# Two attention layers on one core: part of the second layer laid out by another planner's clock, its values joined to the next head's scores, V's weights asked earlier

## The chip, the cores and the metric

One NeuronCore of a Trainium2 chip. The time is device microseconds of one execution of the program. Each kernel is run several times and its median is compared; a profiled execution gives the spans of every instruction.

## The reference

Two independent attention layers on 2048 rows of 1024 numbers, float32, 32 heads of 32. Both project `x` to Q, K and V and the result by `wo`; the two outputs are put side by side.

```python
def _A_ref(x, wqkv, wo):            # W, dil = 8, 2: each row sees itself and 7 rows at steps of two before it
    ...
    idx = pos[:, None] - off[None, :]
    mask = idx >= 0
    ...
    logits = jnp.einsum("bhsd,bhswd->bhsw", q, kg) * scale
    logits = jnp.where(mask[None, None, :, :], logits, -1e9)
    attn = _softmax(logits, axis=-1)
    o = jnp.einsum("bhsw,bhswd->bhsd", attn, vg)
    return (lambda x, *d: x.transpose(*d))(o, 0, 2, 1, 3).reshape(B, S, D) @ wo

def _B_ref(x, wqkv, wo):            # W = 256: each row sees itself and the 255 rows before it
    ...
    scores = jnp.einsum("bhqd,bhkd->bhqk", q, k) * (Dh ** -0.5)
    mask = (idx[:, None] - idx[None, :] >= 0) & (idx[:, None] - idx[None, :] < W)
    scores = jnp.where(mask[None, None], scores, -1e9)
    o = jnp.einsum("bhqk,bhkd->bhqd", _softmax(scores, axis=-1), v)
    ...
```

## The kernel before

The rows come in eight units of 512: units 0 to 3 are layer B ("dense"), units 4 to 7 layer A ("window"; its even and odd rows are separate sequences, so that the dilation becomes a plain window of eight). `DU` is 4, the first unit of layer A. A unit has eight groups of four heads; `hg = 8 * u + s` numbers them through, so layer A has groups 32 to 63. In this text a "head" of layer A is such a group.

**Large matmuls.** Every float32 operand of a projection is split in two fp32r parts (`parts`, L247: a cast on ScalarE or VectorE, L249 or L252, and a subtraction on VectorE, L255), and three products of parts are added, so that one block of contraction is three matmuls of 128x128 by 128x512. A Q/K block `("qk", u, s)` is 2 halves of 8 such steps k, 48 matmuls. V comes in parts: `("v", u, 0)` covers four groups, in two rounds of four weight blocks, 12 matmuls a block. In units 6 and 7 V, and after all units layer A's output, are formed from seven products of sums (`("vp", ...)`, `("p", ...)`), in place of eight. Layer A's sums are made in the background: loads, additions on VectorE (L1073), stores. The items of these products that are sums of inputs are of kind "xw".

**Weights.** The class `Stream` holds all weights and inputs in one list in the order of use. `load_to` fetches the next 512 KB into a raw buffer, by GpSimd's DMA queue (L194), when a split has freed one; `split_to(n)` queues the splits up to item n. Who calls `split_to` and when is set by hand in the blocks: in a Q/K block at certain steps k (L660 to L677), in a V block through `ahead` (L745). Three split weights and three raw buffers are held.

**Small matmuls.** In layer A a head's scores are 64 matmuls of 32x32 by 32x40 in plain float32, each two passes, so 128 matmuls and 128 weight loads. VectorE and ScalarE make the softmax (`mask`, `top`, `total`, L1178 to L1216), transpose it and spread it into `wide` (`spread`, L1218); then the values are 16 or 20 matmuls, 32 or 40 passes. Before, a head's Q and K rows go from TensorE through a buffer (`nat`, three of them) by SyncE's queue into one of two seats (`evac_window`, L555). In the trace the seats bear the name of the buffer that they lie in, `pbuf`.

**The order.** Nothing is decided at run time: a planner in the program text lays out the instructions of every engine. `Clock` (L63) keeps a time for each engine with durations written into it. The loop from L1576 on has four lists: `a` (small helpers), `2` (second passes and values), `1` (scores) and `g` (large matmuls), and takes the item that can start first by the clock. An item's `ready` gives the time from which it can start, or None. Work of the other engines is emitted when the clock reaches it (`defer`).

TensorE's instructions are counted as they are laid out (`issued`; four for a float32 matmul, two for a split one), and `asked` notes when the clock thinks that the next 256 were requested. `short(n)` (L299) says that a burst of n instructions would outrun those that are there; the dispatcher then takes a large matmul instead, if one can start. `Clock.move` (L126) places DMA transfers one after the other on one server.

Of the kernel before, what the change touches and what calls it, by code (L numbers as in the profile page):

```python
# [29 lines left out]
CHUNK, ASKED, LEFT, FETCHED = 256, 150, 290, 7.0  # L30
EXTRA, EACH = 246, 5.2
P_LATE = 1.5
VPARTS = ((0,4),(4,2),(6,2))
V_SLOTS = {0:0,5:1,7:2}
O_SLOTS = {2: (0, 1), 3: (2, 3), 4: (4, 5), 5: (6, 7)}
# [17 lines left out]
CW = 1.36  # L53
# [9 lines left out]
class Clock:  # L63
# [10 lines left out]

    def __init__(self):
        self.free = dict(pe=0.0, act=0.0, dve=0.0, pool=0.0, sp=0.0)
        self.port = dict(dve=0.0, pool=0.0)
        self.later, self.lands, self.busy = [], [], []
        self.n = 0

    @property
# [3 lines left out]
    def start(self, eng, port, *ready):  # L85

        t = max((self.free[eng],) + ready)
        if eng == "pool":
            t = max(t + 0.06, self.port["dve"])
        elif port:  # L90
            t = max(t, self.port["pool"])
        return t
# [4 lines left out]
    def use(self, eng, dur, *ready, port=False):  # L97
        end = self.free[eng] = self.ends(eng, dur, *ready, port=port)
        if eng == "pool" or port:
            self.port[eng] = end  # L100
        return end + self.SEEN[eng]

    def issue(self, eng, kind, *ready):
        start = max((self.free[eng],) + ready) + (0.28 if eng == "pool" else 0.0)
        self.free[eng] = start + self.HOLD[eng]
        return self.move(start + self.LEAD[eng], *self.MOVE[kind])

    def copy(self, kind, *ready):

# [16 lines left out]
    def move(self, t, dur, tail):  # L126

        busy = self.busy = [x for x in self.busy if x[1] > self.now - 20.0]
        i = 0
        while i < len(busy):  # L130
            if busy[i][1] <= t or busy[i][0] < t:
                t = max(t, busy[i][1])
            elif busy[i][0] - t >= dur:
                break
            else:
                t = busy[i][1]
            i += 1
        busy.insert(i, (t, t + dur))
        return t + dur + tail

    def defer(self, t, f):
# [123 lines left out]
def kernel(ctx, tc, xs, wqk, wv, wo, outs, units):  # L265
# [31 lines left out]
        nc.tensor.matmul(out, left, right, **k)  # L297

    def short(n):  # L299
        return ck.now < asked[1] + FETCHED and issued[0] + EXTRA + n > asked[0] * CHUNK + ASKED + LEFT  # L300


    plan = []
# [21 lines left out]
    sx = dram.tile([P, 4, 4, S], F32, name="sx")  # L325
    vd = dram.tile([P, 4, S], F32, name="vd")
    done = {}
    for k in ("stack", "v", "o", "ot", "out", "nat", "second", "clear", "scores", "s", "t", "vs", "vw", "vd"):
        done[k] = {}
    gates = {}  # L330

# [208 lines left out]
    def qk_items(u, s):  # L540
# [14 lines left out]
        def evac_window(t, ps, bank):  # L555
            if t == 0:
                h2["qk"] = natp.tile([P, 2 * S + 16], F32R, tag="nat", name="nat").bitcast(F32)[:, :2 * S + 8]
                nc.scalar.activation(h2["qk"][:, :S], ps, AF.Copy, scale=SCALE)
                e = ck.use("act", 0.485, ck.now + ck.SEM)
                by_head(0, S, e)  # L560
            else:
                qk = h2["qk"]
                nc.scalar.copy(qk[:, S + 8:], ps)
                e = ck.use("act", 0.485, ck.now + ck.SEM)
                nc.scalar.copy(qk[:, S:S + 8], tails[:, s, :])
                e = ck.use("act", 0.2, e)
                if u + 1 < U and not units[u + 1][3]:
                    ck.defer(e + 1.0, lambda: (nc.vector.memset(tails[:, s, :], 0.0), ck.use("dve", 0.08, ck.now)))
                if u + 1 < U and units[u + 1][3]:
                    nc.scalar.copy(tails[:, s, :], ps[:, S - 8:])  # L570
                    e = ck.use("act", 0.2, e)
                by_head(S, 2 * S + 8, e)
            rg.give(bank, e)
# [65 lines left out]
        for t in range(2):  # L639
            h = {}  # L640

            def ready(k, t=t, h=h):
                if k == 0:
                    st.split_to(where["qk", u, s, t] + 1)
                    w = st.ready[where["qk", u, s, t]]
                    h["r"] = w if isinstance(w, list) else [w, w]
                    return latest(rg.when(), h["r"][0], xready[u][0])
                if k >= len(xready[u]):
                    return None
                if k == NK - 1 and nat + t >= NN and (dense or t == 0):  # L650
                    n = done["nat"].get(nat + t - NN)
                    return n and max(xready[u][k], n - 0.6)
                return max(xready[u][k], h["r"][k // 4])

            def run(k, t=t, h=h):
                if k == 0:
                    h["ps"], h["b"] = rg.take()
                    h["w"], _ = st.get(where["qk", u, s, t])
                for i, (a, b) in enumerate(TERMS):
                    mm(h["ps"], h["w"][:, a, k * P:(k + 1) * P], xt[u][k][:, b, :],  # L660
                                     start=(k == 0 and i == 0), stop=(k == NK - 1 and i == 2))
                then = where["qk", u, s, t] + 1
                if t == 1 and s == 0 and u:
                    then = max(then, st.split)
                kinds = [kind for kind, _ in st.items[then:then + 2]]
                if k == ASK and kinds and kinds[0] not in ("x", "xw"):
                    st.split_to(then + 1)
                if k == ASK and t == 0 and u > DU and kinds[:1] == ["x"] and st.split >= where["qk", u, s, 1]:
                    st.split_to(where["qk", u, s, 1] + 1)
                if kinds[:1] == ["xw"] and k in (0, 2, 4, 6):  # L670
                    st.split_to(then + 1 + k // 2)
                if kinds == ["w", "w"] and k == 5 and (then in firsts or then + 1 in firsts):
                    st.split_to(then + 2)
                if kinds == ["w", "xw"] and k == 6:
                    st.split_to(then + 2)
                if k in (4, 6) and kinds[:1] == ["xt"]:
                    st.split_to(then + k // 2)  # L677
                if k == 6 and t == 1 and not hg:
                    st.split_to(7)

            def after(k, t=t, h=h):
                if k == NK - 1:
                    evac(t, h["ps"], h["b"])

            for k in range(NK):
                out.append((lambda k=k, ready=ready: ready(k), lambda k=k, run=run: run(k), 3 * CG,
                            lambda k=k, after=after: after(k)))
# [12 lines left out]
    def v_items(u, part):  # L700
# [11 lines left out]
        def item_of(i):  # L712
            return where["v", u, part, i]
# [12 lines left out]
        def run(r, n, k, b):  # L726
# [15 lines left out]
            done_block = k == kw - 1 and b == 1  # L742
            if wide and r == 0:
                if k == 0 and b == 1 and n < 3:
                    ahead(item_of(n + 1))  # L745
            elif wide:
                if done_block and n == 0:
                    ahead(item_of(4))
                if k == 0 and b == 1 and n == 3:
                    ahead(item_of(4) + 1)  # L750
            elif k == 1 and b == 0:
                ahead(item_of(n) + 1)

        def ahead(i):
            if st.items[min(i, len(st.items) - 1)][0] != "x":
                st.split_to(i + 1)
# [388 lines left out]
    def window(u, s):  # L1145
# [16 lines left out]
        h = {}  # L1162

        def scores_ready():
            return latest(rs.empty(), done["stack"].get((u, s)),
                          done["clear"].get(buf) if hg - 2 <= last_dense else done["o"].get(hg - 2))

        def scores():
# [49 lines left out]
        def spread(e):  # L1218
            turned = band[buf][:, 1024:].rearrange("p (j b t c) -> p j b t c", j=4, b=4, t=2)
            diag = wide[buf].rearrange("p j (b c) -> p j b c", b=4)  # L1220
            for i in range(4):
                r, c = 32 * i, 32 * i + 8
                nc.scalar.copy(diag[r:r + 32, :, :, c:c + 32], turned[r:r + 32, :, :, 1, :])  # L1223
                ck.use("act", 0.632, e)
                n, c = ((i - 1) * 32, c) if i else (96, 0)
                nc.scalar.copy(diag[n:n + 32, :, :, c:c + 8], turned[r:r + 32, :, :, 0, :8])
                h["p"] = ck.use("act", 0.31, e)

        def values_ready():
            return latest(done["v"].get((u, vp)), h.get("p") and h["p"] + P_LATE, ro.when())  # L1230

        def values():
# [10 lines left out]

            return after

        return [Item(scores_ready, scores, CW, 256)], [Item(values_ready, values, C3 + 0.9, 16 * len(kbs))]

    def free_keys(hg):

# [274 lines left out]
            twos += b  # L1524
    xt[0], xready[0] = [], []
    x1 = None
    for p in plan:
        if p[0] == "qk":
            new = qk_items(p[1], p[2])
            if p == ("qk", 0, 0):  # L1530
# [45 lines left out]
    while True:  # L1576
# [16 lines left out]
        if ck.later and (best is None or ck.later[0][0] < best[0]):  # L1593
# [2 lines left out]
            ck.flush(t)  # L1596
            continue
        t, name = best
        it = seqs[name][pos[name]]
        pos[name] += 1  # L1600
        ck.free["pe"] = t
# [49 lines left out]
```

## Time and profile before

| what | value |
|---|---|
| runs | 1799.02, 1805.24, 1803.62 us; median 1803.62 us |
| profiled execution | 1800.08 us, span 1798.4 us |
| TensorE matmul busy | 1775.5 us (99%) |
| VectorE, ScalarE, GpSimd busy | 1298.0, 940.8, 410.6 us |
| layer A's bursts of scores | from 1046 to 1648 us |
| output products | from about 1637 us to the end |

PE is TensorE's matmuls, PEld its weight loads, DVE VectorE, ACT ScalarE, POOL GpSimd, SP SyncE. In the names, `g` is the bank of a large matmul, `s` that of scores and `o` that of values; `x`, `w` and `r` are split inputs, weights and sums (the buffers of the latter have the name `r`). Matmuls overlap in the array, and their ends are modelled by the profiler, so the length of one record is not the time that it costs; the chain of waits and the distance of starts tell that.

### The profile page before, as it was taken

Reading aid. Unit: us, or ns where it says so; the run is one execution under the profiler, and the core shown is the slowest. Engines: PE = TensorE matmul, PEld = TensorE weight load, DVE = VectorE, ACT = ScalarE, POOL = GpSimd, SP = SyncE. Lnnn points to the kernel's source line nnn. Section 1 sums busy time; section 2 is a strip of 40 time slices with the busy share of each in tenths; the row PEclk is TensorE's granted clock in tenths of the full one; section 3 lists DMA queues with packets and bytes.
Section 4 is the critical chain, followed back from the end, with each engine's and each line's share of the span. In section 5 each row is a group of like instructions: output and inputs, shape, how many; then the busy total and the mean of one; then the engine's idle time right before and its main releaser. Section 6 shows DMA issues by size and latency. Waiting matters only on the chain.

```text
span 1798.4 us, 38453 instructions
## 1 busy us (share of the span) xinstructions
PE 1775.5 (99%) x14496; PEld 1440.0 (80%) x14496; DVE 1298.0 (72%) x2887; ACT 940.8 (52%) x2336; POOL 410.6 (23%) x952
## 2 busy tenths in 40 slices
PE   9999999999999999999999999999999999999999
PEld 7787777888777888778788778877887787777887
DVE  6777876768867769867678476756666768689866
ACT  5565566555656565655655444534544435355442
POOL 3322323222342223332223400100010101001120
PEclk9999999999999999999999999999999999999999
DMA  8354664645646556555546265766566568868984
GB/s 257 105 148 136 185 167 135 170 136 141 185 141 166 153 132 170 146 152 149 144 128 173 83 194 180 213 211 186 160 219 203 185 183 280 265 182 270 356 286 144
DMA packets 154794, 324.58 MB, mean 180 GB/s; under 512 B 18032, under 2 KB 58992, under 8 KB 154608
## 3 DMA queue, kind: packets, MB, share of 16 engines
q0 software_dynamic: 45792, 166.74, 30.4%
q1 hardware_dynamic: 98736, 137.02, 26.8%
q10 hardware_dynamic: 10080, 18.35, 2.7%
q8 instruction: 115, 1.88, 0.4%
q14 instruction: 71, 0.58, 0.1%
HBM read 201.33 MB, written 53.48 MB: 142 GB/s over the span
## 4 chain that ended last, share of the span: by engine, by line
PE 89%; DVE 3%; issue 3%; DMA 3%; ACT 2%; POOL 0%; SPq 0%; DVEq 0%; ACTq 0%; POOLq 0%
PE g L297 70%; PE s L297 13%; PE o L297 6%; DMA raw<-xs 1%; DVE w L255 1%; DVE x L255 0%; ACT s L1361 0%; DMA pbuf<-nat 0%; ACT w L249 0%; DVE band L1212 0%; DMA raw<-wqk 0%; DVE sm L1208 0%; DMA qst<-nat 0%; DMA raw<-wv 0%; DVE r L979 0%
## 5 line engine op out<-in xcount | busy, mean ns | idle before, releaser
L297 PE MATMUL g<-x,w 128*128 128x512 f32 x3552 | 879.9, 394 | 4.9 <-DVE x L255 3.1
L297 PEld LDWEIGHTS g<-x,w 128*128 128x128 f32 x3552 | 655.6, 188 | 135.1 <-issue 7.9
L255 DVE TENSOR_TENSOR w<-raw,w 128x512 fp32r<-128x512 f32 x510 | 334.4, 697 | 45.1 <-ACT w L249 39.0
L1361 ACT ACTIVATE s<-s,nm 128x384 f32<-128x384 f32 (+2 forms) x512 | 274.4, 537 | 106.7 <-DVE nm L1356 100.2
L1356 DVE CUSTOM_DVE_ANT_0 s<-s,mask_d 128x384 f32<-128x384 f32 (+2 forms) x512 | 262.0, 554 | 93.1 <-PE s L297 92.8
L297 PE MATMUL g<-w,x 128*128 128x256 f32 (+1 forms) x1728 | 307.7, 327 | 1.3 <-DVE w L255 0.9
L1420 POOL TENSOR_SCALAR_AFFINE_SELECT pbuf<-pbuf 128x128 f32<-128x128 f32 (+1 forms) x603 | 218.8, 391 | 318.9 <-ACT pbuf L1441 317.2
L297 PEld LDWEIGHTS g<-w,x 128*128 128x128 f32 x1728 | 255.3, 190 | 26.4 <-DVE w L255 2.1
L297 PE MATMUL g<-r,w 128*128 128x512 f32 x960 | 239.0, 393 | 1.1 <-issue 0.6
L1441 ACT ACTIVATE pbuf<-s 128x384 f32<-128x384 f32 (+2 forms) x480 | 203.3, 505 | 65.8 <-PE s L297 64.1
L297 PEld LDWEIGHTS g<-r,w 128*128 128x128 f32 x960 | 177.2, 188 | 36.6 <-issue 1.4
L194 POOL DMA_DIRECT2D raw<-wqk x126 | 68.6, 544 | 395.7 <-DVE w L255 256.4
L297 PEld LDWEIGHTS s<-qst,kst 128*128 128x128 f32 x704 | 113.9, 189 | 42.6 <-ACT s L1361 16.8
L297 PE MATMUL s<-kst,qst 96*128 96x384 f32 (+2 forms) x512 | 143.0, 343 | 0.9 <-ACT s L1361 0.7
L297 PE MATMUL s<-qst,kst 128*128 128x256 f32 (+2 forms) x704 | 137.4, 302 | 4.0 <-ACT s L1361 3.2
L252 DVE CAST w<-raw 128x1024 fp32r<-128x1024 f32 x173 | 119.7, 692 | 12.3 <-PE g L297 9.0
L249 ACT CAST w<-raw 128x1024 fp32r<-128x1024 f32 (+1 forms) x83 | 85.8, 1038 | 69.8 <-PE g L297 28.0
L297 PEld LDWEIGHTS s<-kst,qst 96*128 96x128 f32 x512 | 93.7, 189 | 26.6 <-issue 4.4
L1361 ACT ACTIVATION_READ_ACCUMULATOR s<-s,nm 128x1 f32 x512 | 105.3, 206 | 0.0
L1223 ACT COPY wide<-band 32x512 f32<-32x512 f32 x128 | 79.0, 617 | 32.0 <-DVE band L1214 30.4
L297 PE MATMUL o<-pbuf,vbuf 128*32 128x384 f32 (+2 forms) x1408 | 91.1, 388 | 0.0
L255 DVE TENSOR_TENSOR x<-raw,x 128x512 fp32r<-128x512 f32 x116 | 75.4, 689 | 19.8 <-ACT x L249 18.5
(90 smaller groups left out, 1390.8 us busy)
## 6 DMA issues: line engine op xcount, KB each, us to landing
raw<-wqk POOLq DMA_DIRECT2D x126, 512.0 KB, 4.6
raw<-wv POOLq DMA_DIRECT2D x60, 512.0 KB, 4.8
qst<-nat SPq DMA_DIRECT2D x96, 256.0 KB, 6.0
kst<-nat SPq DMA_DIRECT2D x96, 256.0 KB, 5.5
raw<-wo POOLq DMA_DIRECT2D x44, 512.0 KB, 4.3
raw<-xs POOLq DMA_DIRECT2D x28, 512.0 KB, 4.7
outs<-ost ACTq DMA_DIRECT2D x38, 256.0 KB, 3.2
kst<-halo SPq DMA_DIRECT2D x72, 128.0 KB, 4.7
```

Source lines behind the costliest of these rows:

```text
L194: (self.nc.scalar if early else self.nc.gpsimd).dma_start(raw if len(ap.shape) == 2 else raw.rearrange("p (a b) -> p a b", a=2), ap)
L249: nc.scalar.copy(t[:, 0, :], raw)
L252: nc.vector.tensor_copy(t[:, 0, :], raw)
L255: nc.vector.tensor_tensor(t[:, 1, c:c + 512], raw[:, c:c + 512], t[:, 0, c:c + 512].bitcast(F32), op=ALU.subtract)
L297: nc.tensor.matmul(out, left, right, **k)
L1223: nc.scalar.copy(diag[r:r + 32, :, :, c:c + 32], turned[r:r + 32, :, :, 1, :])
L1356: nc.vector.tensor_tensor_reduce(ps[:, :n], ps[:, :n], mask[:, cut:full], scale=-1.0, scalar=BIG, op0=ALU.add, op1=ALU.min, accum_out=nm)
L1361: nc.scalar.activation(ps[:, :n], ps[:, :n], AF.Exp, bias=nm, scale=-1.0, accum_out=sm)
L1420: nc.gpsimd.affine_select(w, w, pattern=[[0, m], [step, n]], compare_op=ALU.is_ge, fill=0.0, base=base, channel_multiplier=chan)
L1441: nc.scalar.activation(w, ps[:, :pack * n].rearrange("p (j n) -> p j n", j=pack), AF.Exp)
```

## The change

It alters the order in which instructions are laid out, and which engine clears a small tile; the arithmetic is the same.

- **Clock.** While the large matmuls from `("qk", 4, 2)` to the first output product are laid out, `ck.traced` is on. GpSimd's own instructions are then placed around the intervals in which VectorE holds the shared port. A transfer goes through `share`: two queues (GpSimd's, and the others), each first in first out; where both have one under way, each moves at half speed. A 512 KB load has a duration of 1.5 us and a tail of 0.76, before 2.12 and 0.14.
- **Joined values.** For heads below `PAIRED` = 50: the scores of a head wait until the probabilities of the head before are spread, and the values of a head wait until the scores of the next are laid out. The scores' instruction count takes in the 64 or 80 of the values.
- **`short`.** More than 7 us after a request it no longer returns "not short" but counts one more packet of 256 as there.
- **V.** In round 0 of `("v", u, 0)`, for units 4 and 5, the split of block n + 2 is asked at block n, before of block n + 1.
- **"xw" items.** Asked at earlier steps of the Q/K block ahead of them.
- **Tails.** In unit 5 the eight clearings of a group's tail columns go from VectorE to GpSimd.

```diff
@@ class Clock
         t = max((self.free[eng],) + ready)
-        if eng == "pool":
+        if eng == "pool" and self.traced:
+            t = next((e for s, e in self.held if s <= t + 0.06 < e), t + 0.06)
+        elif eng == "pool":
             t = max(t + 0.06, self.port["dve"])
...
-        return self.move(start + self.LEAD[eng], *self.MOVE[kind])
+        dur, tail = self.MOVE[kind]
+        if self.traced:
+            return self.share(eng, start + self.LEAD[eng], *((1.5, 0.76) if kind == "load" else (dur, tail)))
+        return self.move(start + self.LEAD[eng], dur, tail)
...
+    def share(self, eng, t, dur, tail):
+
+        mine, other = self.moves[eng == "pool"], self.moves[eng != "pool"]
+        t = begin = max(t, mine[-1][1] if mine else 0.0)
+        for s, e in other:
+            if e <= t:
+                continue
+            n = max(s - t, 0.0)
+            if n >= dur:
+                break
+            t, dur = t + n, dur - n
+            n = min((e - t) / 2, dur)
+            t, dur = t + 2 * n, dur - n
+            if not dur:
+                break
+        mine.append((begin, t + dur))
+        del mine[:-60], other[:-60]
+        return t + dur + tail
...
     def short(n):
-        return ck.now < asked[1] + FETCHED and issued[0] + EXTRA + n > asked[0] * CHUNK + ASKED + LEFT
+        there = asked[0] * CHUNK + ASKED + LEFT + (0 if ck.now < asked[1] + FETCHED else CHUNK)
+        return issued[0] + EXTRA + n > there
...
@@ evac_window
-                    ck.defer(e + 1.0, lambda: (nc.vector.memset(tails[:, s, :], 0.0), ck.use("dve", 0.08, ck.now)))
+                    ck.defer(e + 1.0, lambda: (nc.gpsimd.memset(tails[:, s, :], 0.0), ck.use("pool", 0.08, ck.now)))
...
@@ qk_items, run
-                if kinds[:1] == ["xw"] and k in (0, 2, 4, 6):
-                    st.split_to(then + 1 + k // 2)
+                if kinds[:1] == ["xw"] and k in (0, 2, 4):
+                    st.split_to(then + 2 + k // 2)
...
-                if kinds == ["w", "xw"] and k == 6:
+                if kinds == ["w", "xw"] and k == 3:
                     st.split_to(then + 2)
...
@@ v_items, run
                 if k == 0 and b == 1 and n < 3:
-                    ahead(item_of(n + 1))
+                    ahead(item_of(min(n + 2, 3) if u >= DU else n + 1))
...
@@ window
         def scores_ready():
-            return latest(rs.empty(), done["stack"].get((u, s)),
+            if last_dense + 1 < hg < PAIRED and hg - 1 not in done["p"]:
+                return None
+            return latest(rs.empty(), done["stack"].get((u, s)), done["p"][hg - 1] + P_LATE if last_dense + 1 < hg < PAIRED else 0.0,
                           done["clear"].get(buf) if hg - 2 <= last_dense else done["o"].get(hg - 2))
...
         def values_ready():
+            if hg + 1 < PAIRED and hg + 1 not in done["scores"]:
+                return None
             return latest(done["v"].get((u, vp)), h.get("p") and h["p"] + P_LATE, ro.when())
...
-        return [Item(scores_ready, scores, CW, 256)], [Item(values_ready, values, C3 + 0.9, 16 * len(kbs))]
+        return [Item(scores_ready, scores, CW, 256 + (16 * len(kbs) if hg < PAIRED else 0))], [Item(values_ready, values, C3 + 0.9, 16 * len(kbs))]
...
+        if name == "g":
+            ck.traced = marks[0] <= pos["g"] < marks[1]
```

More of the change, by code (lines that the diff above doesn't have):

```diff
@@ L32 @@
 P_LATE = 1.5
+PAIRED = 50
 VPARTS = ((0,4),(4,2),(6,2))
@@ L76, in __init__ @@
         self.free = dict(pe=0.0, act=0.0, dve=0.0, pool=0.0, sp=0.0)
-        self.port = dict(dve=0.0, pool=0.0)
-        self.later, self.lands, self.busy = [], [], []
+        self.port, self.held, self.traced = dict(dve=0.0, pool=0.0), [], False
+        self.later, self.lands, self.busy, self.moves = [], [], [], [[], []]
         self.n = 0
@@ L100, in use @@
             self.port[eng] = end
+        if port:
+            self.held = [x for x in self.held if x[1] > self.now - 5.0] + [(end - dur, end)]
         return end + self.SEEN[eng]
@@ L327 @@
     done = {}
-    for k in ("stack", "v", "o", "ot", "out", "nat", "second", "clear", "scores", "s", "t", "vs", "vw", "vd"):
+    for k in ("stack", "v", "o", "ot", "out", "nat", "second", "clear", "scores", "s", "t", "vs", "vw", "vd", "p"):
         done[k] = {}
@@ L1226, in spread @@
                 nc.scalar.copy(diag[n:n + 32, :, :, c:c + 8], turned[r:r + 32, :, :, 0, :8])
-                h["p"] = ck.use("act", 0.31, e)
+                done["p"][hg] = h["p"] = ck.use("act", 0.31, e)
         def values_ready():
+            if hg + 1 < PAIRED and hg + 1 not in done["scores"]:
+                return None
             return latest(done["v"].get((u, vp)), h.get("p") and h["p"] + P_LATE, ro.when())
@@ L1526 @@
     x1 = None
+    marks = []
     for p in plan:
+        if not marks and p[1:] == (DU, 2) and p[0] == "qk":
+            marks.append(len(gemm))
+        if len(marks) == 1 and p[0] == "p":
+            marks.append(len(gemm))
         if p[0] == "qk":
```

## The prediction

> **What bounds the kernel now.** I read the page first, then the busy time by stretch, then the waits of TensorE in layer A's attention, then the chain of waits and the timeline around each.
>
> ```profile
> span 1798.4 us, 38453 instructions
> PE 1775.5 (99%) x14496; PEld 1440.0 (80%) x14496; DVE 1298.0 (72%) x2887; ACT 940.8 (52%) x2336; POOL 410.6 (23%) x952
> q8 instruction: 115, 1.88, 0.4%
> PE 89%; DVE 3%; issue 3%; DMA 3%; ACT 2%; POOL 0%; SPq 0%; DVEq 0%; ACTq 0%; POOLq 0%
> 1046.00:1393.00 347.00, 343.66 (x4297) 285.56 (x4300) 226.99 (x409) 157.82 (x295) 36.54 (x65) 1.00 0.63 196
> 1393.00:1541.00 148.00, 141.33 (x1648) 112.25 (x1644) 110.90 (x196) 71.04 (x134) 17.32 (x32) 1.00 0.71 226
> 1541.00:1637.00 96.00, 96.00 (x1478) 76.94 (x1477) 69.43 (x119) 43.18 (x85) 9.92 (x19) 1.00 0.65 200
> ```
>
> The first numbers of a stretch are its length and TensorE's busy time. TensorE (PE) is busy 99% of the span and holds 89% of the chain, so no other engine's busy time is for sale: a change can only remove TensorE's own work or its idle time. The diff removes no matmul. Up to the third Q/K block of unit 4 it changes one thing, how early V's weights are asked in unit 4; the clock is back to the old one where the output products begin, near 1637 us. The stretches between hold 347.00 - 343.66 = 3.3, 148.00 - 141.33 = 6.7 and 0.0 us of idle time: 10.0 us in all. That is the ceiling for every wait that the change could take away; only joined bursts can add to it.
>
> Who ended those waits (1046 to 1669 us; total, times, longest):
>
> ```profile
> PE g L297 <- DVE x L255: 2.9, 2, 2.3
> PE g L297 <- DVE w L255: 2.6, 6, 0.8
> PE g L297 <- issue: 1.6, 2, 1.0
> PE g L297 <- DVE w L252: 1.0, 1, 1.0
> PE o L297 <- issue: 0.9, 1, 0.9
> PE s L297 <- issue: 0.5, 1, 0.5
> PE g L297 <- ACT w L249: 0.4, 1, 0.4
> ```
>
> Two kinds: 2.9 + 2.6 + 1.0 + 0.4 = 6.9 us for a split weight (w) or input (x), and 1.6 + 0.9 + 0.5 = 3.0 us for "issue", which means that nothing in the profile releases TensorE.
>
> **Part 1: values joined to the next scores (heads 32 to 48, 17 joins).** Each burst of small matmuls interrupts the large ones. From the chain of waits (start, length):
>
> ```profile
> 1047.79 6.34 PE g L297 x27
> 1054.14 1.16 PE s L297 x101
> 1055.30 0.52 issue
> 1063.80 1.05 PE o L297 x32
> 1064.85 1.25 PE s L297 x109
> 1079.16 1.25 PE s L297 x109
> 1083.36 1.05 PE o L297 x32
> 1175.25 1.26 PE s L297 x104
> 1176.51 1.10 PE o L297 x32
> 1669.55 124.72 PE g L297 x549
> ```
>
> Undisturbed, one large matmul takes 124.72 / 549 = 0.227 us. The 27 between two bursts took 6.34 rather than 27 x 0.227 = 6.13: 0.21 us goes to leaving and entering. Apart, scores and values cost 1.25 + 1.05 + 2 x 0.21 = 2.72 us; joined, 1.26 + 1.10 + 0.21 = 2.57. A join saves 0.15 us. In the chain four pairs of such bursts already lie against each other (the first at 1063.80, the last at 1356), so 13 joins are new: 13 x 0.15 = **2.0 us**; bounds 0 (the admission rule lets large matmuls in between) and 2.6 (all 17).
>
> The join adds waits: scores of head n+1 wait for the probabilities of head n, and values of n wait for those scores.
>
> ```profile
> 1236.51 1.25 PE s L297 x104
> 1254.45 1.11 PE o L297 x40
> ```
>
> Scores to values of one head took 17.9 us here, and 17 heads in the 347 us stretch make one per 20.4 us, so the chain of one head fits before the next is due. While bursts wait, nothing stands idle: the dispatcher takes large matmuls instead. What is held longer is the seat of a head's Q and K rows and the three buffers before it by at most one head's time. I price that at nothing, since three buffers cover more than one head; if a Q/K block had to wait for its buffer, TensorE would pay directly.
>
> **Part 2: instruction supply.** Three of the "issue" waits lie in heads below 50, one behind it:
>
> ```profile
> 1240.22 1.32 PE L297 MATMUL g<-r,w 128*128 128x512 f32 x5 [0.65 <-issue]
> 1355.66 1.32 PE L297 MATMUL s<-pbuf 32*32 32x40 f32 x128
> 1356.91 0.72 PE L297 MATMUL o<-wide,vbuf 128*32 128x8 f32 x20
> 1358.58 0.88 PE L297 MATMUL o<-wide,vbuf 128*32 128x136 f32 x20 [0.94 <-issue]
> 1483.99 2.88 PE L297 MATMUL g<-x,w 128*128 128x512 f32 x12 [0.97 <-issue]
> ```
>
> All four follow within 3 us of a scores burst: 128 matmuls and 128 weight loads in 1.25 us, where the large ones take 29 us for as many. The instruction queue moved 1.88 MB in 115 packets, and 2 x 14496 instructions over 115 is 252, so a packet is about 256 of TensorE's instructions, one burst. I read these waits as TensorE outrunning that queue. That at 1055.30 is in a second burst 6.34 us behind the first; joined, bursts lie a softmax apart, and it goes (0.5). Those of 0.65 and 0.94 depend on where the burst falls between two packets: the new rule counts values too, and goes on counting after the wait for a packet is over. A pair is 256 + 64 or 80 instructions, though, longer than a packet. Sum 2.1; I take **1.5**, bounds 2.1 and, if pairs starve more than single bursts, well below nothing (the slower rival). The 0.97 lies where heads are no longer joined but the order is new: half, **0.5**.
>
> The Trainium skill (Runtime: NRT & Kernel Launch, Instruction fetch mechanics) also has blocks of 16 KiB, 256 instructions, but says that fetching is mostly hidden because dispatch is slower than the fill. The 0.94 us in the middle of a run that waits for no engine speak against the second half; by that rule this part would be worth nothing, and I take the row.
>
> **Part 3: V asked a block ahead.**
>
> ```profile
> 1172.44 2.81 PE L297 MATMUL g<-w,x 128*128 128x512 f32 x11 [0.66 <-DVE w L255]
> ```
>
> This is unit 5's V, waiting for a split that VectorE put behind a softmax. Asked one block (12 matmuls, 12 x 0.227 = 2.7 us) earlier, it is there: **0.7**, bounds 0 and 0.7. The price: the split can be queued on VectorE or ScalarE before its raw weights landed, with evacuations and softmax behind it. Unit 4's V has the same edit and showed no wait to gain from.
>
> **Part 4: sums and weights of the value products split earlier.** At k = 0, 2, 4 of the Q/K block, with two items at once at k = 0, instead of one at 0, 2, 4, 6; the first of them at k = 3 of the block's first half, not 6.
>
> ```profile
> 1432.17 0.47 PE L297 MATMUL g<-w,r 128*128 128x512 f32 x1 [0.97 <-DVE w L252]
> 1433.41 1.43 PE L297 MATMUL g<-w,r 128*128 128x512 f32 x5 [0.77 <-DVE w L255]
> 1430.01 0.72 POOL L194 DMA_DIRECT2D raw<-wv  x1 [7.55 <-DVE r L255]
> ```
>
> A step of k is three matmuls, 0.7 us, so these come 1.4 to 2 us earlier; each split also frees a raw buffer for the next fetch, and the fetch above waited 7.55 us for just that split. The two waits make 1.7 us, a little more than the shift is sure to cover: **1.2**, bounds 0 and 1.7.
>
> **Part 5: the clock with traced durations.** It changes no instruction, only the order in which they are laid out: a fetch and a hardware transfer now share the engines by halves instead of queueing for one server. What it can gain are the waits left: x 2.9, w 2.6 less 0.7 and 0.8 above, ScalarE's w 0.4, together 4.4 us. The largest:
>
> ```profile
> 1505.49 0.53 POOL L194 DMA_DIRECT2D raw<-xs  x1 [3.51 <-ACT x L249]
> 1511.69 0.62 ACT L249 CAST x<-raw 128x512 fp32r<-128x512 f32 x1 [3.56 <-DMA raw<-xs]
> 1519.55 1.88 PE L297 MATMUL g<-x,w 128*128 128x512 f32 x7 [2.34 <-DVE x L255]
> ```
>
> That fetch took 6.2 us to land and then its split stood behind a softmax on VectorE. A clock that foresees late landings puts other work there, but no data comes sooner: half, **2.2**, bounds 0 and 4.4.
>
> The clearing of eight tails goes from VectorE to GpSimd.
>
> ```profile
> 1305.92 0.07 DVE L568 MEMSET tails<- 128x8 f32 x1 [4.83 <-ACT nat L565]
> ```
>
> VectorE stood 4.83 us for it once, and TensorE has no wait there, so I count nothing. Now GpSimd waits in its place, with the raw fetches of its queue behind it; a fetch late by 4.83 us is the worst.
>
> **The sum.** 2.0 + 1.5 + 0.5 + 0.7 + 1.2 + 2.2 = 8.1 us. Against it stand waits that the new order makes: between 0 (1541 to 1637 had none) and the 10.0 of today's order, which was also laid out ahead; nearer the first, since the known late splits are asked earlier: -1.5. Net 6.6 us. The profiled execution took 1800.08 us, 1.7 more than its span, so 1793.5; the median of the runs is 1803.62, 3.5 above, so 1797.0. I take the middle, **1795.3 us**.
>
> **Rivals.**
> *The waits only move.* Parts 1 to 3 hold (4.7 us), but the new order misfires about as often as the old, so that parts 4 and 5 give at most what new waits take. Gain 0 to 4.7, at the middle 1799.5. For it: the softmax chains, splits and evacuations still go through an in-order VectorE with 227 of 347 us used. Against: the split waits of 0.97, 0.77 and 0.66 us each have an edit of their own.
> *Joined bursts starve TensorE* (slower). Each pair takes 320 to 336 instructions in 2.4 us, more than the packet of 256. One of the two pairs of scores and values that lie together today stalled, 0.94 us; the one at 1175 did not. If all 17 stall so, that is 16.0 us, less the 2.0 + 0.7 + 1.2 + 2.2 - 1.5 = 4.6 that the other parts leave, less 0.5 for the wait at 1055: 10.9 us slower, 1812.8 from the median's and profile's middle (1801.9). It decides from (4.6 + 0.5) / 0.94 = 6 stalling pairs; at (5.1 + 5.4) / 0.94, 12, it can be measured. For it: the row. Against: the admission rule now counts all 336 ahead, and seven us after a packet was asked.
> *"Issue" is not supply.* Then counting buys nothing and part 2 falls out: 6.6 - 2.0 = 4.6 us, 1797.3. That is the rule of the Trainium skill named in part 2. Against it: all four waits lie right behind a burst.
>
> **Chances.** The forecast 0.50; waits move 0.24; starving pairs 0.22, with other ways of lateness that cost as much; the rule of hidden fetching 0.04. A measurement of this kernel tells about 0.3% (5.4 us) from no change; the second and the last case stay within it. So faster 0.50, same 0.28, slower 0.22. The range begins where all idle time and all joins are gained, 1800.08 - 10.0 - 2.0 = 1788, and reaches into the starving case, 1808; the forecast's own is 1789 to 1799.
>
> **What would show it.** Idle time of 1046 to 1393 us under 1.5, of 1393 to 1541 under 4.5; scores and values adjacent 17 times; no wait at the third V block of unit 5; the 0.97 and 0.77 waits gone; fewer "issue" waits. I am wrong if "issue" waits follow the pairs, if the x wait of 2.3 us stays or new split waits appear, or if anything before 970 us differs.

## The result: 6.6 us faster, as forecast, by other parts than priced

| kernel | median us | runs | ratio to before, 95% interval |
|---|---|---|---|
| before | 1802.00 (1798.36 to 1805.24) | 10 | 1 |
| changed | 1795.41 (1792.93 to 1799.47) | 10 | 0.9967 [0.9954, 0.9979] |

The forecast was 1795.3 us, a net gain of 6.6. The profiled execution of the changed kernel took 1796.96 us, with a span of 1795.3.

From its page, and by stretch (length, TensorE's busy time and so on; behind the five engines the granted clock, as a share of TensorE's full clock):

```profile
span 1795.3 us, 38462 instructions
PE 1774.1 (99%) x14496; PEld 1442.2 (80%) x14496; DVE 1297.4 (72%) x2876; ACT 939.9 (52%) x2336; POOL 413.9 (23%) x963
PE 90%; DMA 4%; DVE 3%; issue 1%; ACT 1%; POOL 0%; SPq 0%; DVEq 0%; ACTq 0%; POOLq 0%
1046.00:1393.00 347.00, 342.33 (x4292) 287.06 (x4291) 226.38 (x402) 155.42 (x293) 37.31 (x72) 0.99 0.63 197
1393.00:1541.00 148.00, 146.34 (x1793) 117.47 (x1780) 115.12 (x204) 69.67 (x133) 17.86 (x33) 1.00 0.72 231
1541.00:1637.00 96.00, 96.00 (x1356) 77.23 (x1354) 68.99 (x116) 46.91 (x91) 10.37 (x18) 1.00 0.60 197
1637.00:1669.00 32.00, 30.15 (x320) 23.62 (x319) 27.51 (x46) 23.02 (x41) 5.83 (x11) 1.00 1.00 359
```

The last stretch, which the prediction left out, was this in the kernel before:

```profile
1637.00:1669.00 32.00, 31.82 (x320) 25.41 (x322) 29.88 (x49) 22.65 (x41) 5.73 (x11) 1.00 0.99 349
```

Idle time of TensorE went from 3.3, 6.7, 0 and 0.2 us to 4.7, 1.7, 0 and 1.9: the first and the last stretch became worse, the second much better. In sum it fell from 10.2 to 8.2 us. Who ended the waits from 1046 to 1669 us (total, times, longest):

```profile
PE g L324 <- DVE w L282: 4.9, 6, 2.9
PE g L324 <- DVE w L279: 1.0, 1, 1.0
PE s L324 <- DMA pbuf<-nat: 0.8, 2, 0.6
PE g L324 <- DVE band L902: 0.6, 1, 0.6
PE o L324 <- ACT wide L1256: 0.4, 1, 0.4
PE s L324 <- issue: 0.3, 1, 0.3
```

"Issue" fell from 3.0 us to 0.3, the waits for a split x from 2.9 to nothing. Waits for a split w rose from 4.0 to 5.9, with one of 2.9 us that the kernel before did not have. It is the second row here, the first blocks of unit 5's V; below it, the stretches before, in and after it:

```profile
1158.59 0.39 PE L324 MATMUL g<-w,x 128*128 128x512 f32 x1
1161.86 7.60 PE L324 MATMUL g<-w,x 128*128 128x512 f32 x20 [2.88 <-DVE w L282]
1150.00:1157.00 7.00, 7.00 (x32) 5.77 (x31) 5.38 (x12) 3.58 (x7) 0.72 (x1) 1.00 0.89 292
1158.00:1162.00 4.00, 1.12 (x6) 0.62 (x4) 3.90 (x7) 1.61 (x4) 0.00 (x0) 0.88 0.41 126
1162.00:1169.00 7.00, 7.00 (x19) 5.55 (x20) 4.52 (x8) 4.16 (x9) 2.12 (x4) 0.58 0.71 200
```

After the wait the granted clock is 0.58 of full over seven microseconds, and TensorE, "busy" throughout, starts 19 matmuls where 7 us at 0.227 hold 31. In finer steps the clock is one half for 6.8 us, from 1161.0, 0.8 us before the wait ends. The starts of these matmuls are up to 0.43 us apart; 14 of them cost about 14 x 0.2 = 2.8 us, so in this execution this one late split cost 2.9 + 2.8, nearly as much as the change gained in all. Three of the ten runs had a mean clock of 1.000, where 6.8 us at one half would give 0.998: the wait does not always bring the half clock. VectorE is full in it (3.90 of 4.00 us): the split stood behind the softmax of the head whose scores, from 1143.9 us, had been joined.

The two profiled spans differ by only 3.1 us. The kernels' instructions are the same for the first 970 us, yet in the second profile the blocks from 187 us on stand 1.4 to 1.6 us earlier: the first profile has 3.4 us of half clock near 170 us, the second none there. Sorted by the mean granted clock of the execution, the medians of one program's runs rise in steps:

| mean granted clock | 1.000 | 0.999 | 0.998 | 0.997 | 0.996 |
|---|---|---|---|---|---|
| before, beside the experiments: median us (runs) | 1798.1 (8) | 1800.9 (27) | 1802.0 (27) | 1803.1 (10) | 1805.2 (6) |
| changed: median us (runs) | 1792.9 (3) | 1795.1 (3) | 1797.0 (3) | 1799.1 (1) | |

A step of 0.001 of 1800 us is 1.8 us, about what the columns differ by on average. At equal clock the kernels are 4 to 6 us apart. The mean clock was 0.9988 in the changed kernel's ten runs and 0.9983 in these 78 of the kernel before, which makes another 0.9 us; the rest of the 6.6 is within its interval (3.8 to 8.3 us).

### The profile page after: what moved, and what is told of

Read it like the earlier page. It is cut to its first block, busy times and chain, and to the rows that moved or that the text cites. A ratio compares the mean times of both kernels' runs of the same rounds, so it can differ in the third digit from the quotient of the medians.

```text
span 1795.3 us, 38462 instructions
## 1 busy us (share of the span) xinstructions
PE 1774.1 (99%) x14496; PEld 1442.2 (80%) x14496; DVE 1297.4 (72%) x2876; ACT 939.9 (52%) x2336; POOL 413.9 (23%) x963
## 4 chain that ended last, share of the span: by engine, by line
PE 90%; DMA 4%; DVE 3%; issue 1%; ACT 1%; POOL 0%; SPq 0%; DVEq 0%; ACTq 0%; POOLq 0%
PE g L324 71%; PE s L324 13%; PE o L324 6%; DMA raw<-tv 1%; DMA pbuf<-nat 1%; DVE w L282 1%; DMA raw<-xs 1%; ACT s L1393 0%; DMA sx<-r 0%; DMA outs<-ost 0%; DVE x L282 0%; DMA r<-wo 0%; POOL pbuf L1452 0%; DMA qst<-nat 0%; DVE r L1007 0%
## 5 line engine op out<-in xcount | busy, mean ns | idle before, releaser
L1214 DVE TENSOR_TENSOR band<-s,near 128x160 f32<-128x160 f32 x128 | 32.5, 316 | 87.8 <-PE s L324 81.3
```

What stands on the lines that cost most here:

```text
L1214: nc.vector.tensor_tensor(p64()[:, j, :, 24:], banks[j][0][:, :160].rearrange("p (b c) -> p b c", b=4), m, op=ALU.add)
```

## The experiments

Theory: each part of the change takes away the waits that its rows priced, and the one wait that the new order made was a split queued late. Rivals: the order is drawn anew and waits only move; pairs starve TensorE of instructions; "issue" is not supply. Ratios are to the kernel before, run beside.

| label | what | median us | ratio, interval |
|---|---|---|---|
| a1_no_join | changed, joins undone | 1801.74 | 1.0004 [0.9994, 1.0013] |
| a2_old_clock | changed, clock undone | 1799.51 | 0.9993 [0.9984, 1.0002] |
| a3_v_one | changed, V undone | 1796.72 | 0.9969 [0.9961, 0.9978] |
| a4_xw_old | changed, sums undone | 1802.01 | 0.9998 [0.9984, 1.0012] |
| a5_tails_dve | changed, clearings undone | 1793.94 | 0.9951 [0.9935, 0.9967] |
| b1_join_only | before, joins and admission rule alone | 1801.20 | 1.0001 [0.9992, 1.0009] |
| b2_clock_only | before, clock alone | 1801.48 | 1.0000 [0.9988, 1.0011] |
| d1_no_short | changed, admission rule off | 1817.70 | 1.0092 [1.0073, 1.0110] |
| c1_v_first | changed, one split earlier | 1790.92 | 0.9944 [0.9932, 0.9956] |
| c2_vp_first | and a second one | 1789.99 | 0.9932 [0.9917, 0.9946] |
| c2_again | the same | 1791.92 | 0.9946 [0.9932, 0.9959] |
| c3_both_dve | and clearings undone | 1791.98 | 0.9945 [0.9933, 0.9958] |

**Joins undone.**

```diff
-PAIRED = 50
+PAIRED = 0
```

> The changed kernel with PAIRED = 0: no scores wait for the probabilities of the head before, no values for the next scores; clock, V, sums and tails as changed. Theory 1 (each part gives what its own rows price): the 13 new joins go (each 0.15 to 0.21 us, 2.0 to 2.7) and the waits on 'issue' inside and behind the bursts of heads below 50 come back (2.0 us before): 1795.4 + 4 to 5 = 1799 to 1800, ratio to the kernel before 0.9985. Rival (the order is only drawn anew, waits move): 2.0 to 2.7 us from the entries alone and waits that fall either way, 1793 to 1801, with no more waits on 'issue' than the 0.3 us of the changed kernel.

6.3 us were given back, beyond both. From the waits of that run, its row of a second burst 7.6 us behind the first, and two rows of values:

```profile
PE o L324 <- ACT wide L1256: 3.6, 3, 2.2
PE s L324 <- issue: 3.5, 3, 2.4
1056.71 0.28 PE L324 MATMUL s<-pbuf 32*32 32x40 f32 x10 [2.43 <-issue]
1516.29 1.96 PE L324 MATMUL o<-wide,vbuf 128*32 128x136 f32 x32 [2.25 <-ACT wide L1256]
1529.08 1.12 PE L324 MATMUL o<-wide,vbuf 128*32 128x136 f32 x32 [1.18 <-ACT wide L1256]
```

The wait that measured 0.52 us in the kernel before is 2.43 here, with the new `short` still in force; so the rival, which allowed no more "issue" than 0.3, does not hold whole. But of the other 3.6 us, values laid out before ScalarE had spread the probabilities, 3.4 are the last two rows: heads 54 and 55, which are joined in neither kernel. The stretch of the joined heads (1046 to 1393 us) is idle for 3.1 us, less than the changed kernel's 4.7; the next one for 4.9 rather than 1.7. That part of the loss is the rival's: the order behind the joins was drawn anew. The V of unit 5 has no long wait in this kernel.

**Joins alone.** The edit is the diff's `PAIRED` lines and `short`, on the kernel before.

> The kernel before with the joins and the new admission rule alone (old clock, V, sums, tails). Theory 1: 13 entries saved (2.0 to 2.7 us) and the three 'issue' waits of heads below 50 (2.0 us) gone: 1802.0 - 4 to 5 = 1797 to 1798. Rival (pairs starve): 17 pairs with waits of up to 0.94 us on 'issue', 1802 or more. Rival (waits move): 1802.0 - 2.0 to 2.7, give or take 2.

None of the three: the time did not move. The entries were saved (bursts interrupt the large matmuls 45 times rather than 60) and "issue" fell to 1.6 us in sum, so pairs did not starve. But splits came late, the largest in unit 5's V:

```profile
PE g L298 <- DVE w L256: 7.0, 7, 2.5
PE g L298 <- issue: 1.4, 1, 1.4
1171.22 5.06 PE L298 MATMUL g<-w,x 128*128 128x512 f32 x14 [2.46 <-DVE w L256]
```

7.0 us against 2.6 before for the same kind. Three waits of this run (at 1171, 1344 and 1518 us, all for splits) have 3.4 us of half clock each behind them: the joins' gain was paid back in late splits and in the clock.

**Clock undone.**

```diff
-            ck.traced = marks[0] <= pos["g"] < marks[1]
+            ck.traced = False
```

> The changed kernel with the traced clock never on; joins, V, sums and tails as changed. Theory 1: the waits for split inputs and weights that the clock was credited with come back, about 2 us, above all the 2.3 us for an x near 1516 us: 1797 to 1798. Rival (waits move): within 1.5 us of 1795.4, with waits of about the same sum (5 to 10 us) at other places. If the new clock itself makes the 2.9 us wait at unit 5's V, that wait goes here and the time is 1790 to 1793.

4.1 us lost, twice the price, and at a place near the one named. Unit 5's V has no long wait here, though the heads are joined. The wait at its first block appears only where both the joins and the new clock are in; the kernel with joins alone waits at a later block of that V. Instead, in unit 7's first Q/K block and the value product behind it:

```profile
1513.09 8.12 PE L324 MATMUL g<-x,w 128*128 128x512 f32 x22 [3.75 <-DVE w L282]
1527.97 3.78 PE L324 MATMUL g<-w,x 128*128 128x512 f32 x8 [3.55 <-DVE w L282]
1514.00:1520.00 6.00, 6.00 (x17) 4.67 (x17) 3.79 (x7) 3.86 (x8) 1.06 (x2) 0.57 0.96 345
1527.00:1534.00 7.00, 6.03 (x123) 4.46 (x125) 3.81 (x8) 1.81 (x5) 0.53 (x1) 0.58 0.98 302
```

After each of the two waits the clock was 0.57 to 0.58. No run of this kernel had a mean clock above 0.998; at 0.998 it takes 1798.5 us (four runs), 1.5 behind the changed one, so more than half of the 4.1 us is half clock.

**Clock alone.** The kernel before with the new `Clock` parts and `ck.traced`. The new `short` is in it too, so it is not quite the clock alone.

> The kernel before with the traced clock alone (no joins, V, sums and tails as before). Theory 1 as the prediction priced it: 2.2 us of waits go, 1802 - 2.2 = 1799.8, less new waits. Theory 2, drawn from the runs so far (a part undone from the changed kernel, joins, clock or sums, loses 4 to 7 us, and joins alone gain nothing, so the parts do not add): the clock alone also gains nothing that can be told, 1800.5 to 1803.

Nothing that can be told, the second theory. "Issue" waits are 2.6 us again and the x wait near 1516 us is gone, but another of 2.9 us came near 1527. So neither joins nor clock is worth anything alone, and each is worth 4 to 6 us when the rest is there.

**Sums undone.**

```diff
-                if kinds[:1] == ["xw"] and k in (0, 2, 4):
-                    st.split_to(then + 2 + k // 2)
+                if kinds[:1] == ["xw"] and k in (0, 2, 4, 6):
+                    st.split_to(then + 1 + k // 2)
...
-                if kinds == ["w", "xw"] and k == 3:
+                if kinds == ["w", "xw"] and k == 6:
```

> The changed kernel with the sums and weights of the value products asked at the steps of before. Theory 1: the waits of 0.97 and 0.77 us in the product near 1432 us come back, 1795.4 + 1.2 to 2 = 1796.6 to 1797.4, and 1393 to 1541 us has 3 to 4 us of idle time rather than 1.7. Rival (the clock alone had removed them): within 0.7 us of 1795.4.

6.6 us lost, beyond both. The weights of all three sums products are late:

```profile
1384.11 0.49 PE L324 MATMUL g<-w,r 128*128 128x512 f32 x1 [1.41 <-ACT w L276]
1411.09 0.47 PE L324 MATMUL g<-w,r 128*128 128x512 f32 x1 [0.26 <-DVE w L279]
1438.71 1.65 PE L324 MATMUL g<-w,r 128*128 128x512 f32 x6 [0.82 <-DVE w L282]
```

The stretch from 1393 to 1541 us is idle for 148.00 - 145.57 = 2.4 us, less than theory 1 had. At a mean clock of 1.000 this kernel takes 1796.7 us (two runs), 3.8 behind the changed one; the rest is half clock, down to 1805.7 at 0.996 (median of three).

**V undone.**

```diff
-                    ahead(item_of(min(n + 2, 3) if u >= DU else n + 1))
+                    ahead(item_of(n + 1))
```

> The changed kernel with V asked one block ahead again, in units 4 and 5. As the prediction priced it: unit 5's third V block waits 0.7 us again, 1795.4 + 0.7 = 1796.1. Theory 1 (the 2.9 us wait and the half clock at 1159 us belong to the first block, which was asked at the same step before and after): the wait of the first block stays, the time is 1795.5 to 1797.5. Rival (asking two ahead filled VectorE and made that wait): it goes, and the time is 1790 to 1792.

As expected: 1.3 us more, not told apart from the changed kernel (the intervals overlap); the first block's wait is still there (3.0 us, its longest), so asking V ahead did not make it. The wait at a later block of that V is back too (0.66 us at 1173 us). In this profile the first block's wait has no half clock behind it.

**Clearings undone.** `nc.gpsimd.memset(tails...)` back to `nc.vector.memset`.

> The changed kernel with the eight clearings on VectorE again. Priced at nothing: 1795.4 give or take 1. If VectorE's waits for them (4.8 us once in the kernel before) do delay splits that TensorE needs, up to 2 us slower.

1.5 us less than the changed kernel, with overlapping intervals; c3_both_dve below, beside c2_again, shows no difference.

**Admission rule off.**

```diff
-        return issued[0] + EXTRA + n > there
+        return False
```

> The changed kernel with the admission rule off: a burst is laid out as soon as it is ready, whatever has been counted of TensorE's instructions. If the waits on 'issue' are TensorE outrunning its instruction queue, they come back at the bursts, 0.5 to 2.4 us each in perhaps a third of some 47 bursts: 8 us or more, 1803 or later. If they are not (the recorded rival 'issue is not supply'), the waits stay at about 1 us in sum and the time within 2 us of 1795.4.

22 us slower, and where the supply theory says: in the values of pairs, after most of the pair has run. Its waits, one pair, and the stretch behind that:

```profile
PE o L324 <- issue: 11.9, 6, 2.8
1213.62 1.32 PE L324 MATMUL s<-pbuf 32*32 32x40 f32 x128
1214.86 1.18 PE L324 MATMUL o<-wide,vbuf 128*32 128x8 f32 x38
1218.11 0.41 PE L324 MATMUL o<-wide,vbuf 128*32 128x128 f32 x2 [2.07 <-issue]
1219.00:1223.00 4.00, 4.00 (x12) 3.11 (x11) 2.73 (x4) 1.18 (x2) 0.53 (x1) 0.58 0.19 70
```

Two matmuls short of its end, the pair waits 2.07 us with nothing to release it. Six of the 17 pairs wait so, 11.9 us in all, and at four of them the clock is halved for 3.4 us. The rest of the 22 us is other waits and half clock: TensorE is idle for 20.1 us from 1046 to 1637, against the changed kernel's 6.3. The packets of the instruction queue (q8) in the trace show what these waits are for: each of the six ends 1.3 to 1.6 us after a packet of 16 KB has landed. So do all four "issue" waits of the kernel before, and 18 of the 20 in all profiles that last over 0.3 us from 1010 to 1672 us; a packet comes only every 15.6 us on average. "Issue" is supply. The two others are of 0.6 and 0.4 us at 1645 us with the joins undone, and stay open. The new rule does not keep every such wait away: one of 2.4 us is left with the joins undone, one of 0.99 in c2_vp_first. The Trainium skill (Runtime: NRT & Kernel Launch, Instruction fetch mechanics) calls fetching mostly hidden; that holds for the large matmuls away from bursts here, and not for a burst of 336 instructions in 2.4 us.

**One split earlier.** In the step of the Q/K block:

```diff
+                st.split_to(where["v", 5, 0, 0] + 1) if (u, s, t, k) == (5, 0, 1, 0) else None
```

> The changed kernel with one split asked two steps of k (1.4 us) earlier: the first block of unit 5's V. Its subtraction on VectorE then stands ahead of the second half of a softmax rather than behind it. Theory 1 (the 2.9 us wait at 1159 us, and the half clock of 2.4 to 3 us behind it, are one split that is queued behind a softmax): both go, 1795.4 - 5 to 6 = 1789.5 to 1790.5, and no granted clock below 1 in that stage. Rival (VectorE is simply full there): the wait moves to the next blocks of the same V, 1794 to 1796.

4.5 us gained of the 5 to 6. TensorE's order changed in that V alone; VectorE's, around the split:

```profile
1157.36 1.29 DVE L281 TENSOR_TENSOR w<-raw,w 128x512 fp32r<-128x512 f32 x2
1158.57 0.81 DVE L1238 TENSOR_REDUCE sm<-band 128x16 f32<-128x640 f32 x1
1158.65 3.16 PE L323 MATMUL g<-w,x 128*128 128x512 f32 x13
1163.04 3.24 PE L323 MATMUL g<-w,x 128*128 128x512 f32 x13 [1.23 <-DVE w L281]
1162.00:1169.00 7.00, 5.96 (x169) 4.93 (x173) 6.83 (x15) 3.50 (x8) 1.96 (x4) 1.00 0.72 234
```

The split now stands ahead of the softmax's sums and lets the block begin with 13 matmuls. 1.23 of the 2.88 us moved on to the second block, as the rival had it for the whole; the half clock did not come. Five of this kernel's six runs had a mean clock of 1.000; their median, 1790.8 us, is 2.2 below the changed kernel's at that clock, so about half of the 4.5 us is the half clock that stays away.

**A second split earlier.** `if kinds == ["w", "w"] and k == 5` becomes `k == 3`.

> The kernel with unit 5's first V split asked earlier, and with the second weight of the first value product asked at k = 3 rather than 5 of the Q/K block ahead. Theory 1 (each wait is one split that stands late in VectorE's order): the two waits near 1338 us (1.1 us in sum) go, 1790.9 - 1 = 1790. Rival (VectorE is full there): they move a block on, 1790.5 to 1791.5.

> The fastest version so far once more, beside the other on the same chip: 1789.99 give or take 0.5.

The two waits near 1338 us (0.53 and 0.27 us with the one split earlier) are gone from its profile. Its gain over the one split cannot be told: 0.9932 and, run again, 0.9946 against 0.9944.

**And the clearings back.**

> The fastest version so far (unit 5's first V split and the first value product's second weight asked earlier), with the eight clearings on VectorE again. If the clearings on GpSimd cost something, 1789.99 - 1 to 1.5 = 1788.5 to 1789; if they are worth nothing either way, as priced, 1789.5 to 1790.5.

1791.98 beside 1791.92: worth nothing either way, as priced. The version with both splits earlier beats both kernels: 0.5 to 0.7% under the kernel before, where the change brought 0.3%.

## Why the prediction was right, and where its working was not

The direction, the time (1795.41 for 1795.3) and the net gain came out; that the time came out within 0.1 us is luck, as the steps show:

- **Joins.** All 17 pairs lie together. A pair in the changed kernel's chain:

```profile
1072.07 16.10 PE g L324 x69
1088.17 1.25 PE s L324 x104
1089.41 1.05 PE o L324 x32
1090.47 17.21 PE g L324 x120
```

  1.25 + 1.05 + 0.21 = 2.51 rather than the 2.57 taken from the one pair at 1175 us, so a join saves 0.21 and 13 save 2.7, not 2.0: a little under-sized. Undoing them cost 6.3 us: the entries, the "issue" wait of 2.4, and waits that moved to heads that are joined in neither kernel.
- **Supply.** 1.5 + 0.5 us priced, 2.7 of 3.0 us of waits gone. The starving rival named a real mechanism: without the admission rule six pairs of 17 stall, and each costs more (2.0 us on average, and the clock behind it) than the 0.94 it was priced at. The rule is what held it off, as the text against it said.
- **V ahead.** The 0.66 us at the third block went, as said; on the clock of the runs it cannot be told.
- **Sums earlier.** 0.97 and 0.77 went; 1.2 priced, 6.6 lost without it, of which 3.8 at equal clock.
- **Clock.** The x wait of 2.34 us went; 2.2 priced, 4.1 lost without it.
- **New waits.** Priced at 1.5 us; in the profile the new wait at unit 5's V and its half clock alone took 2.9 + 2.8. This is the step that failed, with its check: the idle time of 1046 to 1393 us was to be under 1.5 and is 4.7; that of the next stretch was to be under 4.5 and is 1.7. New split waits, one of the prediction's own signs of being wrong, did appear. By its terms 1.5 + 0.5 + 0.7 + 1.2 + 2.2 - 1.5 = 4.6 us of idle time were to go; 2.0 went.
- **Half clock.** No term had it, though it decides how dear a wait is.

The net was right because errors cancel: 2.0 us of idle time for 4.6, against joins of 2.7 for 2.0 and a somewhat better clock, which no term had. Undone one at a time, joins, clock, V and sums lose 6.3 + 4.1 + 1.3 + 6.6 = 18.3 us, far over the 6.6 that all bring; joins or clock alone bring none. So the sum of parts, as the prediction made it, was no valid working for a laid-out order. The idle time from the first burst to layer A's last values says the same: 10.2 us before and 8.2 changed; 10.8, 10.7, 10.6 and 10.2 with joins, clock, V or sums undone; 11.9 and 10.1 with joins or clock alone; 4.7 with one split earlier. The "waits move" rival is right about a single part. For all of them its highest gain, 4.7 us, is what entries and idle time give here (2.7 + 2.0), and lies within the interval of the 6.6, so it is not refuted either. Why together they leave fewer waits is shown by place (which split or burst is late in which kernel), not by a rule that would foretell it; that stays open.

## What to carry to other kernels

Where the bounding engine idles 0.6% of the span, look for single late operations in an in-order queue: one split moved ahead of half a softmax was worth 4.5 us, about half of it at equal clock, where no part was forecast above 2.2. Price a wait of two to four microseconds on TensorE with the clock that it may halve, compare runs at equal granted clock before crediting an edit, and compare idle time in sum, not only the waits that went. Join small bursts only with a count of the instructions that are there: the same pairs were 6 us of gain with the count and 22 us of loss against that without it.

## What the runs showed of the hardware that was not expected

- Waits of 2.07 us (d1_no_short) and 2.88 us (changed) came with a granted clock of one half for 3.4 and 6.8 us; the kernel before had one of 2.34 us at 1519 us that did not. In the fourteen profiles TensorE waited 21 times for 1.9 us or more between 1046 and 1669 us: at 17 of them half clock began, between 1.9 us before and 1.4 us after the wait's end, and lasted 3.4 or 6.8 us. Of the 16 waits of 1.0 to 1.9 us two were followed by it. The same wait at unit 5's V (2.8 to 3.0 us) had 6.8 us of half clock in the changed kernel, 3.4 with the sums or the clearings undone, and none with V undone. The Trainium skill (TensorE: Matmul & The Clock Gate, HAM oscillation) advises against idle gaps over some 3.4 us, and says (in What's actually happening) that the clock gate's window is 3.4 us long and runs freely. The second agrees with the lengths of the spells, and with one wait that met them in some kernels and not in another; the first is too lenient here, since 15 of the 17 waits were shorter.
- TensorE can run out of instructions: up to 2.77 us at a time, here only in bursts of small matmuls or within 4 us behind them. Eighteen of twenty such waits ended 1.3 to 1.6 us after the next packet of the instruction queue had landed.
